# A Fourier transform with a soft mixture of experts behind it: one product of 128 columns along a, loads in halves, and another explicit order

## The chip, the core and the metric

The kernel runs on one core of a Trainium2 chip, in float32. The metric is the device time of one execution in microseconds. TensorE (PE; its weight loads are listed as PEld), VectorE (DVE), ScalarE (ACT), GpSimd (POOL) and SyncE (SP, which issues every DMA here) each work through a queue of their own in order and wait for each other by semaphores. Products go to PSUM, which has 8 banks of 512 floats per partition, and DVE or ACT have to copy them out.

## The reference

```python
x: (8, 2496, 256); phi: (256, 32); w1: (8, 256, 1024); w2: (8, 1024, 256)
x = np.fft.fft(np.fft.fft(x, axis=1), axis=2).real.reshape(19968, 256)
logits = x @ phi                                   # 19968 x 32 slots
d = softmax of logits over the 19968 tokens        # with + 1e-9 below the sum
slot_input = (d.T @ x).reshape(8, 4, 256)
slot_out[e] = np.maximum(slot_input[e] @ w1[e], 0) @ w2[e]
c = softmax of logits over the 32 slots            # with + 1e-9 below the sum
return c @ slot_out.reshape(32, 256)               # 19968 x 256
```

Nothing can be written before the last token has been read: the softmax over tokens needs the largest logit and the sum of all of them. So there is a stage that loads (x, then the expert weights) and one that stores.

## The kernel before

The 8 batches are worked in 4 pairs, p = 0 to 3. The 2496 tokens of a batch are 64 values a times 39 values c, so that the transform along the sequence is a small product along a and another along c. Step names below are a letter code and numbers (pair, tile or half), as they stand in `PLAN`, and each names a function.

- `X` (`load_x`) loads one of five tiles of x of a pair, 1 MB each (896 KB for the first), into one of six 1 MB homes R0 to R5. `XT` (`load_turned`) does it for a copy of pair 3 that is laid out turned. `F`, `G`, `H` (DVE, L302 and L313) fold a tile's mirrored tokens and features into a home E.
- `T` and `A` turn a tile on PE (L318) and copy it out of PSUM; `Zo`, `Ze`, `Zt` multiply with the phi tables (L333, L351), `Y` copies, `t` turns (L372), and `y` (`turn_z_copy`, L377) copies the turned z, slot by slot, into a home M.
- `a` (`along_a`, L394) is the product along a, `b` its copy, `l` (`along_c`, L410) the products with cosines and sines along c, in two halves of the groups. `L` copies the cosine product of a half, `M` and `N` (L428, DVE) add and subtract the sine product from PSUM: these are the logits.
- `R`, `V`, `v`, `vb`, `W`, `w` find each slot's largest logit of the pair, `E` (ACT, L463) the exponentials, `q` (DVE) their sums and differences. `e` (L480) and `d` (L494) go back along c and a, `u` (`inputs`, L522) multiplies with the folded x.
- After all four pairs `ac` (DVE), `acT`, `at`, `si`, `sT` put the slot inputs together, `h` (L610, w1), `r`, `x`, `s` (L628, w2), `so`, `rep` (L638) give the expert outputs. `I` and `J` load w1 (1 MB each, homes R) and w2 (512 KB each, homes E).
- For the outputs, `O` and `Q` (L648) turn the logits back to tokens, `ca`, `cb`, `cc`, `cd`, `ce` do the softmax over slots (DVE, ACT, some on POOL), `lT` and `lc` turn its weights (L693), `po` (`product`, L711) multiplies, `ev` copies out of PSUM into the homes R, and `S` (L723) stores 384 KB to 1 MB.

What sets the order is `PLAN` alone, a list of some 860 steps written out in full: it is walked once from front to back, each step issues its instructions on its engines, `/a`, `/v` or `/g` names the engine of a copy (ACT, DVE, POOL), and `=name:home` says which buffer a result takes. So an engine's queue has its steps in the list's order, and a load stands in SP's queue until the home that it names is free.

Of the kernel before, what the change touches and what calls it, by code (L numbers as in the profile page):

```python
# [8 lines left out]
F32 = mybir.dt.float32  # L9
# [8 lines left out]
D = 256  # L18
# [8 lines left out]

DIRECT = ()
# [5 lines left out]
X03=x03:R0 C0 F03 G03=e03:E0 T030=bT030:B0 X04=x04:R1 A030/a=et010:E1 H03 T031=bT031:B1 A031/a=et011:E2 X01=x01:R2  # L34
F04 G04=e04:E3 T040=bT040:B2 X00=x00:R3 H04 F01 A040/a=et020:E4 H01=e01:E5 T041=bT041:B3 T011=bT011:B4 C1
A041/a=et021:E6 A011/a=et001:E7 F00 P H00=e00:E8 phi=bphi:B5 T001=bT001:B6 A001/a wphi G01 Zo02=bz02:B7
T010=bT010:B0 A010/a=et000:E9 G00 T000=bT000:B1 Zo00=bz00:B2 X02=x02:R4 A000/a Ze00 F02 H02=e02:E10 T021=bT021:B3
A021/a G02 T020=bT020:B4 A020/a Ze02 X13=x13:R5 Zo01=bz01:B5 Ze01 Y02/a=zs0:M0 X14=x14:R0 C2 Y00/a F13 wneg
H13=e13:E11 G13 Y01/a t00=bt00:B6 y00/a=zt0:M1 t02=bt02:B0 X10=x10:R1 X11=x11:R2 y02/a F14 G14=e14:E12 H14
t01=bt01:B1 T130=bT130:B3 T131=bT131:B4 y01/a a02=ba02:B7 X12=x12:R3 F10 b02/a=oo0:M2 a01=ba01:B2 A131/a=et111:E13  # L40
b01/a a00=ba00:B5 A130/a=et110:E14 l01=bl01:B6,bm01:B0 L01/a=lt0:M3 X20=x20:R4 H10=e10:E15 T101=bT101:B1 b00/a
A101/a=et101:E16 T140=bT140:B7 T141=bT141:B4 A141/a=et121:E17 G10 A140/a=et120:E6 T100=bT100:B2 M01 F11 X21=x21:R5
N01 H11=e11:E7 l00=bl00:B3,bm00:B6 Zo12=bz12:B5 G11 Ze12 T111=bT111:B1 F12 O02=bc02:B4 L00/a A100/a=et100:E9 M00
Y12/a=zs1:M4 t12=bt12:B0 T110=bT110:B7 A111/a Zo10=bz10:B3 H12=e12:E4 X24=x24:R0 A110/a Ze10 X22=x22:R1 G12 Y10/a
T121=bT121:B2 X23=x23:R2 A121/a T120=bT120:B5 t10=bt10:B1 F20 N00 H20=e20:E2 Zo11=bz11:B7 A120/a Ze11 R01
O01=bc01:B3 y10/a=zt1:M5 y12/a Q02/a=c0:M6 T201=bT201:B2 Y11/a R00 t11=bt11:B6 y11/a V01=bv01:B5 O00=bc00:B1 G20
T200=bT200:B0 A200/a=et200:E1 XT30=xt30:R3 F24 Q01/a A201/a=et201:E17 Q00/a v01 V00=bv00:B4 vb01/a=me01:X0
a11=ba11:B7 v00 vb00/a=me00:X1 a10=ba10:B6 G24=e24:E6 b10/a=oo1:M7 b11/a H24 a12=ba12:B0 b12/a XT32=xt32:R4
XT34=xt34:R0 W01 T240=bT240:B3 A240/a=et220:E16 T241=bT241:B2 W00 l11=bl11:B1,bm11:B6 F21 F22 A241/a=et221:E9
L11/a=lt1:M8 w00/a l10=bl10:B7,bm10:B0 w01/a L10/a E001=d00:D0 Zo22=bz22:B3 G21=e21:E13 H21 Ze22 Y22/a=zs2:M9  # L50
H22=e22:E14 T211=bT211:B2 F23 A211/a M10 T221=bT221:B1 T210=bT210:B4 A210/a t22=bt22:B5 y22/a=zt2:M0 FT30 M11
Zo20=bz20:B7 H23=e23:E9 Ze20 Zt30=bz30:B3 E000 Y20/a A221/a=et211:E16 N11 XT33=xt33:R5 T231=bT231:B2 G22 N10 A231/a
t20=bt20:B4 T220=bT220:B5 XT31=xt31:R3 A220/a=et210:E17 O10=bc10:B7 O12=bc12:B6 O11=bc11:B1 G23 E011=d01:D1
Q11/a=c1:M1 R11 V11=bv11:B0 T230=bT230:B2 FT34 Zo21=bz21:B5 A230/a Ze21 Y21/a Zt34=bz32:B1 y20/a Q10/a Y32/a=zs3:M2
Q12/a E010 FT32 Zt32=bz31:B2 FT33 Zt33 Y31/a FT31 Zt31 Y30/a R10 V10=bv10:B5 v11 vb11/a=me11:X0 q010=q01:D2
t21=bt21:B4 t31=bt31:B7 v10 C3 q001=q00:D3 q011 ca00 vb10/a=me10:X1 t30=bt30:B1 y21/a y31/a=zt3:M4 y30/a cb00/v q000
C4 X31=x31:R1 W10 w10/a E100=d10:D1 W11 t32=bt32:B6 a21=ba21:B2 y32/v F31 E101 G31=e31:E1 J1=w21:E16 w11/v
q100=q10:D0 ca01 q101 a22=ba22:B3 b22/a=oo2:M5 b21/a a20=ba20:B4 b20/a e00=be000:B7,be001:B1 e01=be010:B5,be011:B6
# [36 lines left out]
po32=bp320:B1,bp321:B6,bp322:B4,bp323:B0 ev131/a S300 ev331/a ev320/v=o32:R0 ev323/a S110
po31=bp310:B3,bp311:B7,bp312:B5,bp313:B2 ev312/v=o31:R2 ev313/v ev311/a ev322/a
# [724 lines left out]
```

## Time and profile before

| | before |
|---|---|
| median of 3 runs | 183.2 us (182.17 to 184.05) |
| the profiled execution | 183.17 us, of it 181.4 us span from the first to the last instruction |
| busy: PE, DVE, ACT | 143.6, 127.0, 111.9 us |
| moved by DMA | 64.29 MB, mean 354 GB/s over the span |
| granted TensorE clock, mean | 0.918 |

The profile is one execution on the chip. The chain of waits is the work that ended last, followed back from the end: a piece is an engine's work, a DMA, or "issue", which is time in which the engine waited for nothing that the profile shows. A busy time is the union of an engine's instructions; PE's ends are modelled.

### The profile page before, as it was taken

What the parts mean: (1) busy time and instruction counts of PE and PEld (TensorE: products, weight loads), DVE (VectorE), ACT (ScalarE), POOL (GpSimd) and SP (SyncE); (2) the same over time, 40 slices, a digit from 0 to 9 for tenths busy, and PEclk for the clock granted to TensorE, in tenths of its full rate; (3) what the DMA queues carried; (4) which work ended last, traced back from release to release, by engine and by line L of the source; (5) the groups of instructions that cost most, each with busy time, mean ns of one, the idle gap of its engine ahead of it and who ended that gap; (6) DMA issues with size and microseconds to landing.
All of it is one profiled execution on the core that took longest, in us unless ns stands there. A gap on an engine that the chain in (4) does not pass through costs nothing.

```text
span 181.4 us, 5827 instructions
## 1 busy us (share of the span) xinstructions
PE 143.6 (79%) x2494; PEld 99.6 (55%) x2494; DVE 127.0 (70%) x222; ACT 111.9 (62%) x268; POOL 11.4 (6%) x24
## 2 busy tenths in 40 slices
PE   0279969998999993999963999999999989796000
PEld 0257658668788882766951386448575745342000
DVE  0699893998999794969977086997899777343000
ACT  2042677798997995879962453545877877545100
POOL 2000000000000000000000000002855000000000
PEclk9999999999999999999997599999999999955555
DMA  5999999999858999851799925799999999999994
GB/s 193 426 417 419 413 421 416 423 420 386 302 206 354 425 423 409 351 175 42 246 388 412 417 74 219 264 401 407 405 400 374 405 419 424 414 426 416 423 416 206
DMA packets 11546, 64.29 MB, mean 354 GB/s; under 512 B 1409, under 2 KB 1793, under 8 KB 6401
## 3 DMA queue, kind: packets, MB, share of 16 engines
q1 hardware_dynamic: 11520, 63.93, 88.2%
q8 instruction: 19, 0.31, 0.7%
q14 instruction: 7, 0.05, 0.1%
HBM read 43.48 MB, written 20.45 MB: 352 GB/s over the span
## 4 chain that ended last, share of the span: by engine, by line
PE 65%; DMA 9%; ACT 7%; issue 6%; DVE 4%; SPq 0%; ACTq 0%; DVEq 0%
PE B L711 10%; PE B L318 7%; PE B L494 6%; PE B L394 6%; DMA out<-R 6%; PE B L333 6%; PE B L522 5%; ACT M L235 5%; PE B L628 4%; PE B L610 4%; DMA R<-xh 4%; PE B L480 4%; PE B L410 3%; PE B L693 3%; PE B L648 2%
## 5 line engine op out<-in xcount | busy, mean ns | idle before, releaser
L235 ACT COPY M<-B 128x480 f32<-128x480 f32 (+11 forms) x101 | 44.2, 524 | 17.5 <-PE B L480 6.0
L235 ACT COPY R<-B 128x512 f32<-128x512 f32 (+1 forms) x49 | 25.3, 592 | 12.0 <-PE B L711 6.6
L711 PE MATMUL B<-E,rh 32*128 32x512 f32 (+2 forms) x192 | 29.8, 589 | 2.8 <-ACT R L235 1.6
L235 ACT COPY E<-B 128x512 f32<-128x512 f32 (+1 forms) x37 | 21.1, 583 | 16.4 <-PE B L318 15.1
L233 DVE COPY R<-B 128x512 f32<-128x512 f32 (+1 forms) x31 | 19.7, 664 | 12.9 <-PE B L711 6.9
L302 DVE TENSOR_TENSOR R<-R 128x1024 f32<-128x1024 f32 (+1 forms) x20 | 23.1, 1163 | 7.2 <-DMA R<-xh 6.9
L318 PE MATMUL B<-cs,E 128*128 128x128 f32 x120 | 20.1, 316 | 9.0 <-DVE E L313 9.0
L313 DVE TENSOR_TENSOR E<-R 128x512 f32<-128x512 f32 x40 | 26.2, 682 | 0.7 <-PE B L522 0.4
L711 PEld LDWEIGHTS B<-E,rh 32*128 32x128 f32 x192 | 15.4, 193 | 13.6 <-ACT R L235 8.6
L318 PEld LDWEIGHTS B<-cs,E 128*128 128x128 f32 x120 | 15.9, 162 | 12.2 <-DVE E L313 10.2
L463 ACT ACTIVATE D<-M,nm 124x128 f32<-124x128 f32 x44 | 14.2, 400 | 0.0
L480 PE MATMUL B<-cs,D 60*64 60x60 f32 x352 | 7.4, 222 | 7.3 <-issue 7.3
L394 PE MATMUL B<-cs,M 128*64 128x64 f32 x352 | 11.4, 223 | 2.2 <-issue 1.4
L428 DVE TENSOR_TENSOR M<-M,B 124x320 f32<-124x320 f32 (+1 forms) x16 | 8.0, 513 | 7.0 <-ACT M L235 6.9
L394 PEld LDWEIGHTS B<-cs,M 128*64 128x64 f32 x352 | 10.8, 138 | 4.0 <-issue 4.0
L333 PE MATMUL B<-E,wphi 128*32 128x256 f32 (+1 forms) x216 | 12.1, 359 | 0.0
L494 PE MATMUL B<-M,cs 128*32 128x320 f32 x128 | 11.9, 529 | 0.0
L687 POOL TENSOR_TENSOR M<-M,cm 128x640 f32<-128x640 f32 x5 | 6.3, 1264 | 86.7 <-DVE cm L682 86.7
L480 PEld LDWEIGHTS B<-cs,D 60*64 60x64 f32 x352 | 6.5, 135 | 8.5 <-issue 8.2
L522 PE MATMUL B<-E,M 128*32 128x129 f32 x320 | 9.9, 274 | 0.7 <-issue 0.7
L522 PEld LDWEIGHTS B<-E,M 128*32 128x32 f32 x320 | 8.8, 110 | 1.4 <-issue 0.9
L468 DVE TENSOR_TENSOR D<-D 124x320 f32<-124x320 f32 (+1 forms) x16 | 7.8, 512 | 1.8 <-ACT D L463 1.8
(94 smaller groups left out, 169.8 us busy)
## 6 DMA issues: line engine op xcount, KB each, us to landing
R<-xh SPq DMA_DIRECT2D x16, 1024.0 KB, 12.0
out<-R SPq DMA_DIRECT2D x12, 1024.0 KB, 9.6
E<-w2h SPq DMA_DIRECT2D x16, 512.0 KB, 8.1
R<-w1h SPq DMA_DIRECT2D x8, 1024.0 KB, 8.1
out<-R SPq DMA_DIRECT2D x9, 512.0 KB, 4.4
R<-xth SPq DMA_DIRECT2D x4, 1024.0 KB, 5.6
R<-xh SPq DMA_DIRECT2D x4, 896.0 KB, 11.9
out<-R SPq DMA_DIRECT2D x3, 896.0 KB, 6.6
```

The lines of the kernel that those rows point to most:

```text
L233: v.tensor_copy(dst, src)
L235: sc.copy(dst, src)
L302: v.tensor_tensor(x[:, lo], x[:, lo], x[:, hi], op=ALU.add)
L313: v.tensor_tensor(d, x[:, 0:4, 0:128], x[:, 0:4, 128:256], op=ALU.subtract if k else ALU.add)
L318: pe.transpose(b[:, g * 128 : g * 128 + 128], x[:, g, k * 128 : k * 128 + 128], ident)
L333: pe.matmul(z[32 * g : 32 * g + 32, o : o + n], wphi[:, w, :], turned_x(p, u, k)[:, g].rearrange("p h q a -> p (h q a)"), start=w != 0, st ...
L394: pe.matmul(d[64 * r : 64 * r + 64, h, i], z[:, 4 * b + i, h], C("wa")[:, 64 * r : 64 * r + 64], start=True, stop=True, tile_position=(0, ...
L463: sc.activation(d[:, g], L[:, g], AF.Exp, bias=nms[:, p, hf, g : g + 1], scale=1.0)
L480: pe.matmul(b[64 * k : 64 * k + 64, 60 * i : 60 * i + 60], q[rows, i, m if direct else k], C(tab)[rows], start=m == 0, stop=m == 1 or not ...
L494: pe.matmul(b[32 * c : 32 * c + 32, :320], C("wb")[:, 64 * k + 32 * (c % 2) : 64 * k + 32 * (c % 2) + 32], s[:, 16 * hf : 16 * hf + 16, c ...
L522: pe.matmul(b[32 * g : 32 * g + 32, 0:129], d[:, k, c, :], x[:, c % 4, 0:129] if k == 0 else x[:, c % 4, 127:256], start=cc == 0, stop=cc ...
L711: pe.matmul(view(f"bp{p}{b}{i}", 512)[:, q * n : q * n + n], rh[rows, dc], l[rows, :n], start=True, stop=True, tile_position=(32 * i, 0),)
```

## The change

The product along a is issued once for each group of three slots, over 128 columns of the whole table, where there were four products of 64 columns by 64. Its rows now hold the halves h, and its columns the cosine and sine parts r, so the products along c take their rows by h. The sine product lands with its halves exchanged; it is copied to SBUF, half by half, and the sums are made against the cosine product in PSUM. The copy of the turned z walks its columns so that runs of 8 (or 4) neighbours are written, and reads PSUM in steps instead. Loads of x, of the turned x and of w1 are halves of what they were, each a step of its own. Fourteen products of a tile of ones with itself (`dm`) are put at places of the list, and the list is another one throughout.

```diff
+WARM = (256, 256, 256, 256, 256, 256, 256, 256, 256, 256, 256, 256, 256, 256)
 PLAN = """
-X03=x03:R0 C0 F03 G03=e03:E0 T030=bT030:B0 X04=x04:R1 A030/a=et010:E1 H03 T031=bT031:B1 A031/a=et011:E2 X01=x01:R2
...
+dm11=bw11:B0 dm3=bw3:B1 dm13=bw13:B2 X011=x01:R0 C0 X010 X030=x03:R1 F01 H01=e01:E0 G01 X031 F03 G03=e03:E1
...
+        warm = const("warm", 128, max(WARM)) if WARM else None
...
+        def keep_warm(e, i):
+            n = WARM[i]
+            pe.matmul(view(f"bw{i}", 512)[:, :n], warm[:, :128], warm[:, :n], start=True, stop=True)
...
-        def load_x(e, p, t):
+        def load_x(e, p, t, h):
             r0, n = _rows(t)
-            nc.sync.dma_start(view(f"x{p}{t}", n * D), xh[p, :, r0 * D : (r0 + n) * D])
+            lo, hi = (0, 4) if h == 0 else (4, n)
+            nc.sync.dma_start(view(f"x{p}{t}", n * D)[:, lo * D : hi * D], xh[p, :, (r0 + lo) * D : (r0 + hi) * D])
...
+        def load_w1(e, i, h):
+            src = w1h[i // 4, i // 2 % 2, i % 2][:, 2 * h : 2 * h + 2]
...
-            d = z[:, :, :, :60].rearrange("p g h (s c) -> p h c g s", s=GS)[:, :, 8 * u : 8 * u + 4 * nq]
-            b = view(f"bt{p}{u}", 512)[:, : 256 * nq].rearrange("p (h i s) -> p h i s", h=2, s=NSLOT)
-            copy(e, d[:, :, :, : NG - 1], b[:, :, :, :30].rearrange("p h i (g s) -> p h i g s", s=GS))
-            copy(e, d[:, :, :, NG - 1, :2], b[:, :, :, 30:])
+            d = z[:, :, :, :60].rearrange("p g h (s c) -> p g s h c", s=GS)[:, :, :, :, 8 * u : 8 * u + 4 * nq]
+            b = view(f"bt{p}{u}", 512)[:, : 256 * nq].rearrange("p (h i s) -> p s h i", h=2, s=NSLOT)
+            copy(e, d[:, : NG - 1], b[:, :30].rearrange("p (g s) h i -> p g s h i", s=GS))
+            copy(e, d[:, NG - 1, :2], b[:, 30:])
 
         def along_a(e, p, b):
...
-                for h in range(2):
-                    for r in range(2):
-                        pe.matmul(
-                            d[64 * r : 64 * r + 64, h, i], z[:, 4 * b + i, h], C("wa")[:, 64 * r : 64 * r + 64],
-                            start=True, stop=True, tile_position=(0, 64 * r),
-                        )
+                g = 4 * b + i
+                pe.matmul(
+                    d[:, i * 128 : i * 128 + 128], z[:, g].rearrange("p h q -> p (h q)"), C("wa"), start=True, stop=True
+                )
...
         def along_c(e, p, hf):
             g0, n = GH[hf]
             for h in range(2):
+                rows = slice(64 * h, 64 * h + 60)
                 for r in range(2):
-                    o = view(f"oo{p}", 2, NG, NA)[64 * r : 64 * r + 60, h, g0 : g0 + n].rearrange("p u k -> p (u k)")
-                    b = view(f"b{'lm'[r]}{p}{hf}", 512)
+                    o = view(f"oo{p}", 2, NG, NA)[rows, r, g0 : g0 + n].rearrange("p u k -> p (u k)")
+                    b, c = view(f"b{'lm'[r]}{p}{hf}", 512), 64 * (h ^ r)
...
-        def along_c_copy(e, p, hf):
-            g0, n = GH[hf]
-            b = view(f"bl{p}{hf}", 512, rows=124)[:, : n * NA]
-            copy(e, logits(p, hf)[:, :, 0], b.rearrange("p (g n) -> p g n", g=n))
+        def along_c_copy(e, p, hf, h):
+            n = GH[hf][1]
+            lo, w = 64 * (1 - h), (64, 60)[h]
+            b = view(f"bm{p}{hf}", 512)[lo : lo + w, : n * NA]
+            copy(e, logits(p, hf)[64 * h : 64 * h + w, :, 0], b.rearrange("p (g n) -> p g n", g=n))
...
-            v.tensor_tensor(L[:, :, 1 - i], L[:, :, 0], b, op=ALU.subtract if i else ALU.add)
+            v.tensor_tensor(L[:, :, 1 - i], b, L[:, :, 0], op=ALU.subtract if i else ALU.add)
```

**How the order moves, on PE, where pair 0 starts its way back.** Before, PE's queue from the turned z of pair 3 (L372) through the product along a of pair 2 (L394) into the way back along c of pair 0 (L480):

```order
L453 MATMUL B_104<-cs_112,X_102 124x128
L372 MATMUL B_110<-cs_112,M_90 128x128 x2
L394 MATMUL B_106<-cs_114,M_88 64x64 x16
L394 MATMUL B_107<-cs_114,M_88 64x64 x12
L394 MATMUL B_108<-cs_114,M_88 64x64 x16
L480 MATMUL B_111<-cs_115,D_101 64x60 x2
L480 MATMUL B_105<-cs_115,D_101 64x60 x2
```

The last two rows repeat: both halves of pair 0's way back stand there in a row, 44 products in all, each of which is two matmuls in the profile.

After, on the same engine, around the first half of pair 0's way back (L490; L329 is `T`, L383 is `t`, L344 is `Zo` and `Ze`):

```order
L383 MATMUL B_111<-cs_112,M_97 128x128 x4
L329 MATMUL B_106<-cs_112,E_84 128x128 x4
L383 MATMUL B_109<-cs_112,M_97 128x128 x2
L329 MATMUL B_105<-cs_112,E_84 128x128 x4
L383 MATMUL B_104<-cs_112,M_88 128x128 x2
L344 MATMUL B_110<-E_87,wphi 32x256 x8
L344 MATMUL B_110<-E_83,wphi 32x256 x4
L490 MATMUL B_106<-cs_115,D_99 64x60 x2
L490 MATMUL B_108<-cs_115,D_99 64x60 x2
```

Only the first half, 24 products, stands there now, behind turns and products of other pairs; the second half follows some 180 matmuls later.

**On ACT, pair 0's turned z and logits.** Before, the six copies of `y` (M_89 from PSUM), those of the product along a, and the one copy that a half of the logits has (M_91):

```order
L235 COPY M_89<-B_110 128x2x8x10x3
L235 COPY M_89<-B_110 128x2x8x2
L235 COPY M_89<-B_104 128x2x4x10x3
L235 COPY M_89<-B_104 128x2x4x2
L235 COPY M_89<-B_105 128x2x8x10x3
L235 COPY M_89<-B_105 128x2x8x2
L235 COPY M_90<-B_111 128x2x192
L235 COPY E_83<-B_108 128x8x64
L235 COPY M_90<-B_106 128x2x256
L235 COPY E_84<-B_107 128x8x64
L235 COPY M_91<-B_110 124x5x64
```

After, from the second copy of `y` on:

```order
L242 COPY M_89<-B_104 128x10x3x2x4
L242 COPY M_89<-B_104 128x2x2x4
L242 COPY M_89<-B_106 128x10x3x2x8
L242 COPY M_89<-B_106 128x2x2x8
L242 COPY M_90<-B_109 128x2x256
L242 COPY M_90<-B_107 128x2x256
L242 COPY M_90<-B_105 128x2x192
L242 COPY M_91<-B_111 128x2x2x64
L242 COPY M_92<-B_106 64x6x64
L242 COPY M_92<-B_106 60x6x64
```

As many copies of `y` as before, with 8 or 4 neighbours innermost instead of 3 or 2 columns apart, and two copies for a half of the logits (M_92) where one was.

**On SP, the last loads before the stores.** Before, then after (L257 and L270 are w1, L262 and L273 w2):

```order
L257 DMA R_65<-w1h 128x2048
L257 DMA R_68<-w1h 128x2048
L257 DMA R_64<-w1h 128x2048
L257 DMA R_67<-w1h 128x2048
L262 DMA E_73<-w2h 128x1024
```

```order
L270 DMA R_69<-w1h 128x1024
L273 DMA E_79<-w2h 128x1024
L270 DMA R_66<-w1h 128x1024 x2
L270 DMA R_65<-w1h 128x1024 x2
L273 DMA E_76<-w2h 128x1024
```

A w1 load is now two of 512 KB; behind the last of w1 there were seven loads of w2, and there are six.

## Rows read from the trace of the kernel before

**Rows 1.** Busy time by stretch: start:end, length, busy us of each engine, clock, DMA share, GB/s.

```profile
0.00:126.30 126.30, 106.38 (x2148) 77.79 (x2149) 98.86 (x174) 82.58 (x211) 1.86 (x17) 0.97 0.86 337
126.30:181.40 55.10, 37.22 (x348) 21.84 (x348) 28.13 (x49) 29.36 (x58) 9.57 (x8) 0.79 0.97 394
70.00:80.00 10.00, 8.15 (x221) 6.33 (x221) 5.83 (x11) 6.28 (x18) 0.00 (x0) 1.00 0.74 282
90.00:100.00 10.00, 5.54 (x184) 4.00 (x179) 7.64 (x14) 4.63 (x13) 0.00 (x0) 0.86 1.01 395
100.00:110.00 10.00, 10.00 (x216) 6.41 (x208) 4.38 (x8) 5.36 (x14) 0.00 (x0) 0.80 0.63 242
```

**Rows 2.** SP's timeline, the last loads and the stores: start, us, line, tiles, count.

```profile
116.21 8.22 SPq L262 DMA_DIRECT2D E<-w2h  x7
128.22 43.14 SPq L723 DMA_DIRECT2D out<-R  x25
```

**Rows 3.** The chain of waits in order of time: start, us, what.

```profile
25.29 1.40 issue
26.68 2.79 PE B L394 x88
...
38.36 1.28 ACT M L235 x3
...
59.29 1.40 ACT M L235 x5
...
66.88 1.42 PE B L480 x85
68.30 2.85 issue
...
80.35 3.91 PE B L494 x56
...
91.50 1.52 PE B L522 x45
93.02 1.42 PE B L480 x83
94.44 3.80 issue
...
98.71 7.06 PE B L494 x64
...
126.29 2.00 PE B L711 x16
```

**Rows 4.** The page's DMA queues: packets, MB, share of 16 engines.

```profile
q8 instruction: 19, 0.31, 0.7%
...
HBM read 43.48 MB, written 20.45 MB: 352 GB/s over the span
```

**Rows 5.** ACT by form, 23.1 to 27.5 us, pair 0's turned z: count, busy us, mean ns.

```profile
L235 ACT COPY M<-B 128x480 f32<-128x480 f32 x2 | 2.5, 1266 | 0.0
L235 ACT COPY M<-B 128x240 f32<-128x240 f32 x1 | 0.8, 781 | 0.0
```

**Rows 6.** ACT by form, 111.9 to 115.5 us, turned logits; then a half of the logits.

```profile
L235 ACT COPY M<-B 128x480 f32<-128x480 f32 x2 | 1.1, 565 | 0.0
L235 ACT COPY M<-B 128x240 f32<-128x240 f32 x1 | 0.4, 361 | 1.5 <-PE B L648 1.5
...
L235 ACT COPY M<-B 124x384 f32<-124x384 f32 x4 | 1.9, 478 | 0.2 <-PE B L410 0.2
```

**Rows 7.** The chain of waits, dense runs of 128-by-128 matmuls, turn and product.

```profile
34.79 0.44 PE B L318 x4
...
125.53 0.29 PE B L638 x2
```

**Rows 8.** Busy time by stretch as above: loads of 512 KB, then stores of 1 MB.

```profile
122.00:127.00 5.00, 4.96 (x118) 4.13 (x114) 4.05 (x8) 2.75 (x5) 1.07 (x1) 1.00 1.01 401
160.00:170.00 10.00, 6.30 (x17) 2.22 (x14) 3.27 (x5) 3.90 (x8) 0.00 (x0) 0.50 1.01 421
```

**Rows 9.** What DVE's folds waited for, in total, times, longest.

```profile
DVE R L302 <- DMA R<-xh: 6.9, 3, 5.8
```

More of the change, by code (lines that the diff above doesn't have):

```diff
@@ L39 @@
[L39 to L58, printed above, removed]
@@ new lines @@
+l01=bl01:B4,bm01:B7 Zo11=bz11:B2 A130/a Ze11 L011/a X101 F10 L010/a Y11/a M00 G10=e10:E4 H10 T100=bT100:B6
+T101=bT101:B5 X110=x11:R3 X111 F11 H11=e11:E6 G11 t11=bt11:B3 A101/a=et101:E7 N00 M01 T111=bT111:B1 A111/a
+T110=bT110:B7 O00=bc00:B2 R00 A110/a=et100:E9 A100/a Zo10=bz10:B5 Ze10 V00=bv00:B0 y11/a Y10/a N01 X240=x24:R4
+X201=x20:R5 X200 F20 v00 vb00/a=me00:X0 G20=e20:E5 O02=bc02:B1 Q02/a=c0:M6 H20 O01=bc01:B7 t10=bt10:B6 y10/a Q00/a
+X211=x21:R0 X210 X241 F21 F24 G21=e21:E2 W00 T200=bT200:B4 T201=bT201:B3 A200/a=et200:E13 a10=ba10:B5 b10/a=oo1:M7
@@ new lines @@
+Y31/a b22/v l20=bl20:B3,bm20:B4 L200/a=lt2:M9 v11 vb11/a=me11:X1 L201/a l21=bl21:B6,bm21:B5 L210/a q010=q01:D0 q011
+X301=x30:R1 e01=be010:B1,be011:B7 f011/a L211/a f010/a X340=x34:R3 X341 F34 q101=q10:D1 W11 t31=bt31:B0 y31/a
+G34=e34:E7 M20 w11/v q100 E111=d11:D2 t30=bt30:B4 y30/a E110 N20 d000=bd000:B7 D000/a d011=bd011:B2 D011/a
+d010=bd010:B5 D010/a M21 e10=be100:B1,be101:B3 R20 V20=bv20:B0 f100/a=es1:M2 X311=x31:R4 a31=ba31:B4 b31/a=oo3:M4
+N21 R21 a32=ba32:B6 f101/v J0=w20:E17 X331=x33:R5 X320=x32:R2 q110=q11:D0 v20 H34 q111 ca00 vb20/a=me20:X0
@@ new lines @@
+a30=ba30:B7 b32/a V21=bv21:B2 W20 l31=bl31:B3,bm31:B5 X321 e11=be110:B1,be111:B4 C4 J1=w21:E13 w20/v X300 b30/a
+L311/v=lt3:M5 l30=bl30:B6,bm30:B7 u00=bu0:B0 u01 u02 u03 u04 L310/a f110/a f111/a L300/a M31 N31 v21 L301/a
+vb21/a=me21:X1 E201=d20:D3 E200 d101=bd101:B5 d100=bd100:B1 R31 V31=bv31:B4 W21 D100/a=ds1:M0 D101/a w21/a U0/a
+E210=d21:D1 X330 X310 I21=w12:R0 M30 N30 O31=bc31:B3 R30 q200=q20:D2 V30=bv30:B7 q201 e20=be200:B6,be201:B1
+f200/a=es2:M3 I40=w14:R3 E211 F32 d110=bd110:B5 d111=bd111:B2 v30 v31 vb31/a=me31:X0 H32=e32:E8 D110/a
@@ new lines @@
+s14 po02=bp020:B1,bp021:B7,bp022:B0,bp023:B4 lc10/v=ls10:E2 ev023/a=o02:R5 ev022/a J15=w215:E5 J13=w213:E13 ev020/a
+s15 ev021/a cb11/g ce31/g cd30 po10=bp100:B3,bp101:B2,bp102:B4,bp103:B6 ev101/v=o10:R3 s16 s17 ev100/a S001
+lT02=bl02x:B0 dm6=bw6:B1 so1/a ev102/a ev103/v rep1=br1:B7 dm7=bw7:B2 lc02/a=ls02:E9 rh1/a ce20/v cd21
+po04=bp040:B3,bp041:B5,bp042:B6,bp043:B1 po01=bp010:B4,bp011:B0,bp012:B7,bp013:B2 ev041/a=o04:R4 ev043/a
+ev011/a=o01:R2 ev042/v S000 ev040/v ev010/v ev013/v lT32=bl32x:B6 lc32/v=ls32:E0
@@ new lines @@
+po03=bp030:B5,bp031:B1,bp032:B3,bp033:B0 ev012/a cc11 ev033/a=o03:R1 cd11 ev031/v S021 lT20=bl20x:B4 ev030/a
+lc20/a=ls20:E11 ev032/a dm0=bw0:B7 dm10=bw10:B2 po34=bp340:B6,bp341:B0,bp342:B7,bp343:B5 ev340/a=o34:R0
+po21=bp210:B2,bp211:B4,bp212:B1,bp213:B3 ev342/a ev343/a S020 ev341/v ev210/a=o21:R5 ev212/v ev213/v ce30/g
+dm1=bw1:B6 po20=bp200:B0,bp201:B7,bp202:B5,bp203:B6 S100 ev202/a=o20:R3 S041 ev200/a ce11/g ce21/v ev203/v
+lT22=bl22x:B1 S010 lT30=bl30x:B2 ev211/v lc22/a=ls22:E1 S011 S040 S030 S031 po24=bp240:B3,bp241:B5,bp242:B6,bp243:B0
@@ new lines @@
+ev242/v=o24:R2 ev240/a dm9=bw9:B1 lT11=bl11x:B4 ev241/a lc30/a=ls30:E12 S340 ev201/a S210 S200 lT12=bl12x:B1
+lT31=bl31x:B6 dm2=bw2:B3 lT21=bl21x:B5 ev243/v po31=bp310:B0,bp311:B2,bp312:B3,bp313:B7 lc21/a=ls21:E3
+lc11/v=ls11:E6 lc12/v=ls12:E4 ev312/a=o31:R4 ev310/a ev313/a dm8=bw8:B4 lc31/v=ls31:E10 S240 ev311/v
+po32=bp320:B1,bp321:B6,bp322:B5,bp323:B4 ev320/a=o32:R1 ev321/a po12=bp120:B3,bp121:B2,bp122:B0,bp123:B7
+ev123/a=o12:R0 ev121/a ev323/v ev322/v ev122/v ev120/v po13=bp130:B1,bp131:B4,bp132:B6,bp133:B5 ev131/a=o13:R5
@@ new lines @@
+ev132/a ev130/v po14=bp140:B7,bp141:B0,bp142:B2,bp143:B3 ev142/a=o14:R3 ev141/v ev143/a ev140/v
+po11=bp110:B4,bp111:B1,bp112:B6,bp113:B2 ev110/v=o11:R2 S120 ev112/a ev113/v dm12=bw12:B0 dm4=bw4:B3
+po23=bp230:B7,bp231:B0,bp232:B6,bp233:B3 ev230/v=o23:R0 S140 S310 ev111/a ev133/a S130
+po30=bp300:B1,bp301:B4,bp302:B5,bp303:B2 ev302/v=o30:R3 ev301/v ev231/a ev232/a ev303/a ev233/a S230
+po33=bp330:B0,bp331:B6,bp332:B7,bp333:B2 ev332/v=o33:R4 ev333/a ev331/a po22=bp220:B3,bp221:B2,bp222:B5,bp223:B6
@@ L101 @@
+ev330/a ev223/a=o22:R5 S330 S110 S320 ev222/a ev300/a ev220/a ev221/a S300 S220
 """.split()
@@ L401, in along_a_copy @@
             s, d = view(f"ba{p}{b}", 512)[:, : 128 * n], view(f"oo{p}", 2, NG, NA)
-            copy(e, d[:, :, 4 * b : 4 * b + n], s.rearrange("p (h u k) -> p h u k", h=2, u=n))
+            copy(e, d[:, :, 4 * b : 4 * b + n], s.rearrange("p (u r k) -> p r u k", u=n, r=2))
         def along_c(e, p, hf):
@@ L406, in along_c @@
             for h in range(2):
+                rows = slice(64 * h, 64 * h + 60)
                 for r in range(2):
-                    o = view(f"oo{p}", 2, NG, NA)[64 * r : 64 * r + 60, h, g0 : g0 + n].rearrange("p u k -> p (u k)")
-                    b = view(f"b{'lm'[r]}{p}{hf}", 512)
+                    o = view(f"oo{p}", 2, NG, NA)[rows, r, g0 : g0 + n].rearrange("p u k -> p (u k)")
+                    b, c = view(f"b{'lm'[r]}{p}{hf}", 512), 64 * (h ^ r)
                     pe.matmul(
-                        b[64 * h : 64 * h + 64, : n * NA], C(("wcc", "wcs")[r])[64 * r : 64 * r + 60], o,
-                        start=True, stop=True, tile_position=(64 * r, 64 * h),
+                        b[c : c + 64, : n * NA], C(("wcc", "wcs")[r])[rows], o,
+                        start=True, stop=True, tile_position=(64 * h, c),
                     )
@@ L746, in _build @@
         with tc.manual_schedule():
+            if WARM:
+                gp.memset(warm, 1.0)
             gp.memset(mneg, 0.0)
@@ L754, in _build @@
                     at_home[name] = home[where_]
-                args = [int(i) for i in parts] if kind != "J" else [int(parts)]
+                args = [int(i) for i in parts] if kind not in ("J", "dm") else [int(parts)]
                 kinds[kind](e, *args)
```

108 lines of the change are left out of this document (46 added, 62 removed).

## The prediction

> **What bounds the kernel now.** I read the busy times by stretch first. They split at 126.3 us, where the first product for the outputs starts [rows 3]. Behind it the 16 DMA engines are busy 0.97 of the time [rows 1]: the stores go out from 128.22 us on [rows 2], 20.45 MB [rows 4], and at the 421 GB/s of a stretch of stores [rows 8] that is 48.6 us of the 53.2 that are left of the span; most of the rest is late w2, issued from 116.21 us on. So the end is the first store plus a fixed amount, and PE (37.2 us busy of 55.1), DVE (28.1) and ACT (29.4) have room there. What the change is worth is what it does to the first product.
>
> Up to 126.3 us nothing is full: PE 106.4 us, DVE 98.9, ACT 82.6, DMA 0.86 [rows 1]. The chain of waits tells where the time between goes. Three kinds of piece in it are not PE's own work:
> - PE waits for ACT around the turned z: 1.40 us at 25.29 (listed as "issue", but ACT's copies of pair 0's turned z end there), and further pieces near 38 and 59 us [rows 3].
> - PE stops for 2.85 us at 68.30 and 3.80 us at 94.44, both in the middle of the way back along c (L480), behind matmuls of the same step that wait for nothing [rows 3].
> - After the second stop the clock falls: the granted mean is 0.86 and 0.80 in the two stretches around it [rows 1], and 64 matmuls of L494 take 7.06 us where 56 took 3.91 before [rows 3]; 64 at that pace are 4.47, so 2.6 us are lost.
>
> I take the two stops for instruction fetch. PE's instructions come by DMA: queue q8 moved 0.31 MB in 19 packets [rows 4], 16.3 KB each, and 2494 matmuls ([rows 1], two of them counted in both stretches) with as many weight loads are 262 instructions, 131 matmuls, per packet. By the order of before, the stops lie 637 matmuls apart, 4.9 packets. And each comes where PE runs fastest: the last 128 matmuls before the first are 85 of L480 in 1.42 us and 43 of L394 at 2.79/88 us, 2.78 us together; before the second, 45 of L522 in 1.52 us and 83 of L480 in 1.42, 2.94 us [rows 3]. With the stop, a packet needed 5.6 and 6.7 us there, with the data queue full (share 1.01 in the stretch with the second, [rows 1]).
>
> The Trainium skill, "Runtime: NRT & Kernel Launch", section "Instruction fetch mechanics", says that blocks of 256 instructions are fetched by the sequencer's own queue while the current one runs, and that this is hidden by the issue floor. The packet size agrees; that it is hidden does not fit these stops. By the page they have another cause, which is a rival below.
>
> **Part by part.**
>
> *Turned z in runs.* The copy of 480 columns takes 1266 ns and that of 240 takes 781 [rows 5], while copies of the same shapes that write neighbours and read PSUM in steps, as the new form does, take 565 and 361 [rows 6]. I take the latter: 0.70 and 0.42 us less, 12 copies, 7.3 us of ACT. On the path are pair 0's three (1.8 us, but the wait was 1.4), two of 480 and one of 240 in the piece near 38 (1.8), and three of 480 near 59 (2.1): 5.3 us. The bounds are 0, should it be the reading in long steps that costs, and 5.3. I take 5.3 since only the write side differs between the two groups of rows.
>
> *Sine products copied in halves.* 16 copies instead of 8, 0.48 us each [rows 6]: +3.8 us of ACT, net -3.5 with the above. The sums wait for both halves, so on the path it is one such copy at pair 1 and one at pair 3, about -0.9 us; bounds 0 and -3.8.
>
> *Product along a.* 88 matmuls in 2.79 us per pair [rows 3] become 22 of full size. At the pace of the turns, 0.44/4, these are 2.42 us, and at that of the only 128-by-128 product, 0.29/2, 3.19 [rows 7]: over four pairs from 1.5 us gained to 1.6 lost. I take +1.0, nearer to the turns, since they too stand in a run. More weighty are 264 matmuls fewer, that is two packets of instructions.
>
> *The stops.* The order decides here. In the list after, matmul 983 (the first stop's) has 128 matmuls ahead of it that are 5.8 us of PE at the paces above (products along a, turns, half a way back), not 2.8: that stop is covered. Matmul 1620 falls among `k` and `si`, with 3.5 us ahead of it, mostly L522: up to 6.7 - 3.5 = 3.2 us remain, where PE waits for DVE's gather anyway; I leave 1.5. With 0.4 for the first, of 2.85 + 3.80 + 2.6 = 9.2 us some 7.3 are won. Bounds: 0 (both return) to 9.2.
>
> *Loads in halves.* A fold needs both halves, so nothing starts sooner. In a stretch of 512 KB loads DMA moves 401 GB/s at a share of 1.01, against 421 [rows 8]: 5%. Up to about 45 us loads follow each other without a gap, so at most 2 us; but behind the first tile DVE's folds waited 6.9 - 5.8 = 1.1 us for them in all [rows 9], so I take -0.5. The Trainium skill speaks against this edit: "DMA: Bandwidth & Descriptors", section "Bandwidth", wants transfers of 1 MiB and more, and fits about 2 us fixed per transfer. If that stood in line, 33 more transfers would be 66 us; the rows at 401 GB/s show transfers overlapping, so my sum doesn't use it.
>
> *Products of ones.* Four stand ahead of the first turn, while PE waits for the first tile: nothing. Ten stand at the expert outputs or later: 20 matmuls at 0.11 to 0.145 us, 2.2 to 2.9 us of PE behind or beside the first products, where DMA is the bound. Nothing, and if that cover were gone 2.9. The clock in the stretch before them they cannot change.
>
> *DVE's queue.* By steps of the list DVE does 2.5 us more ahead of the first product (two copies of turned x, a copy of weights, two subtractions of softmax maxima; others left). That is no delay by itself, but it is the next limit.
>
> **The sum.** 5.3 - 0.9 + 1.0 + 7.3 - 0.5 = 12.2 us earlier by the terms. I do not take all of it, since with these waits gone DVE is next. It was idle 126.3 - 98.9 = 27.4 us: 5.8 for the first tile [rows 9], 4.2, 2.4 and 5.6 in the three stretches with the stops and the slow clock [rows 1], and 9.4 in small waits that I let stand. Then the first product can't come before 98.9 + 2.5 + 5.8 + 9.4 = 116.6, 9.7 us earlier. The loads are 43.5 MB [rows 4], at 401 GB/s 108 us, so DMA too has only some 8 us left to wait for free homes. I take 118.6, 7.7 us earlier: **175.5 us** for the profiled execution (183.17), which is the median (183.2) within 0.1.
>
> **Rivals.**
> - *More.* All of the 12.2 us comes, DVE's small waits shrinking with ACT's load: 171. For it: ACT has 7 us less to do ahead of the first product. Against: PE, DVE and DMA would all be nearly full at once.
> - *The stops are not fetch*, as the page has it, and stay with the way back along c, which is as long as before: 12.2 - 7.3 = 4.9 us, or 178.3 to 180. Against: they came in two of eight ways back, five packets apart.
> - *The next limit takes all.* DVE's 2.5 us, the halved loads (up to 2 us) and pair-by-pair waits of the new order fill what ACT and PE gave: within 1%, 181.4 to 185.
> - *Slower.* The stops return at worse places: the list after has a run of both halves of pair 3's way back with L522 behind, 128 matmuls in 3.0 us, and one from L522 to the first w1 products in 3.1. If a packet ends in each with the queue full, that is 6.7 - 3.0 and 6.7 - 3.1, and 2.6 to 3.3 us of half clock behind each: 13.3 against 9.2 now, 4 us more; the full clock of the products along c would go as well. With the strided reads costing what the strided writes did (5.3 not won), the sine copies on the path (up to 3.8) and the loads' 2 us it is 187 to 191. It decides from about 3 us of new stops on, if ACT's gain fails too.
> - *The change doesn't do what it says:* the reads of PSUM in steps of 128 bytes could cost as the writes did; then the 5.3 us go, and 179 to 181 is left. I count it with the second rival.
>
> **How the numbers follow.** A difference of 1% (1.8 us) is about what a measurement of this kernel can tell from no change. Chances: forecast (173 to 178.2) 0.46, more (under 173) 0.14, fetch or strided reads otherwise (178.3 to 181.3) 0.14, the next limit takes all 0.14, slower 0.12. Faster by over 1%: 0.46 + 0.14 + 0.14 = 0.74; within 0.14; slower 0.12. The range 171 to 184.5 leaves out the slower case and the ends of two others, about 0.18.
>
> **What would show it.** The 480-column copies of the turned z near 0.57 us; the products along a near 2.4 us per pair; no "issue" of over 1 us within the way back along c, and a granted clock of 1.00 up to the first product; that product near 118 to 119 us with DVE over 100 us busy before it; 17 or 18 packets on q8; DMA at 0.97 behind it and stores of the same length. I am wrong if the copies stay over 1 us, if PE stops again where L522 and the ways back meet, or if the first product moves and the end doesn't.

## The result and the profile after

| | before | after |
|---|---|---|
| median of 10 runs | 183.0 us (181.91 to 185.68) | 180.92 us (176.53 to 181.99) |
| ratio after/before | | 0.9703 (0.9619 to 0.9787) |
| second set, 6 runs | 183.14 us | 181.14 us (180.4 to 183.79), ratio 0.9887 (0.9840 to 0.9933) |
| profiled execution | 183.17 us, span 181.4 | 181.21 us, span 179.3 |

The first ratio rests on the two shortest of the ten executions, since the others were counted as disturbed; the medians of all ten, and the second set, give 0.989, and I take that: some 2 us faster. The forecast was 7.7 us faster.

Busy time by stretch after (start:end, length, busy us of PE, PEld, DVE, ACT and POOL, clock, DMA share, GB/s), cut at the gather (where PE starts to put the slot inputs together, L571 before and L581 after) and at the first product, to be held against [rows 1]:

```profile
0.00:102.50 102.50, 89.41 (x1596) 67.09 (x1596) 85.27 (x142) 70.45 (x192) 1.67 (x17) 0.97 0.97 369
102.50:123.75 21.25, 17.54 (x348) 11.08 (x347) 16.88 (x35) 8.44 (x21) 5.51 (x4) 1.00 0.77 278
123.75:179.30 55.55, 37.37 (x323) 20.60 (x322) 27.22 (x51) 30.20 (x61) 3.79 (x3) 0.84 0.91 371
```

and the same two stretches of before, up to the gather and from there to the first product:

```profile
0.00:110.60 110.60, 90.76 (x1853) 68.67 (x1853) 84.83 (x140) 75.30 (x192) 1.49 (x16) 0.97 0.86 340
110.60:126.30 15.70, 15.62 (x297) 9.12 (x296) 14.03 (x34) 7.29 (x19) 0.37 (x1) 1.00 0.82 320
```

The gather starts 8.2 us earlier than before (102.5 against 110.7), and up to it DMA has been busy 0.97 of the time, against 0.86 before. Then 5.7 of these go again: the way to the first product takes 21.25 us where it took some 15.6, and PE, which had next to no idle time there, now waits 3.7. The rest to the end is as long as before (55.6 against 55.1).

The chain of waits after, from where PE stopped before to the gather and on (start, us, what):

```profile
83.88 0.92 issue
...
88.66 0.96 PE B L490 x53
89.62 3.17 issue
92.79 0.81 PE B L490 x35
93.60 1.02 PE B L532 x16
94.62 3.32 PE B L504 x32
...
103.65 1.53 issue
...
106.75 0.93 PE B L620 x6
...
108.46 10.24 DMA R<-w1h
118.70 0.04 issue
118.74 1.06 PE B L620 x8
```

Of the two stops in [rows 3] the first is gone. PE stops in pair 3's way back still (now L490), but after 53 matmuls, 3.17 us long, with a granted clock of 0.67 from 92.79 to 97.94 us: 32 matmuls of L504 take 3.32 us where 16 took 1.1. By the count of matmuls, which the shift below explains, this is not the second stop of before; that one is the 1.53 us at the slot inputs. And the last product with w1 waits for a load, by PE's list of waits:

```profile
PE B L620 <- DMA R<-w1h: 1.9, 1, 1.9
```

The copies of the turned z of pair 0 (ACT by form, 22 to 29 us: count, busy us, mean ns), the counterpart of [rows 5], and the queues of the page, of [rows 4]:

```profile
L242 ACT COPY M<-B 128x480 f32<-128x480 f32 x2 | 1.1, 562 | 0.0
...
L242 ACT COPY M<-B 128x240 f32<-128x240 f32 x1 | 0.4, 363 | 0.0
```

```profile
q1 hardware_dynamic: 16272, 63.94, 91.8%
q8 instruction: 18, 0.29, 0.6%
```

The copies are as fast as was read from [rows 6]. The data queue's packets took 91.8% of 16 engines over 179.3 us, 164.6 us; before it was, in the same place of the page:

```profile
q1 hardware_dynamic: 11520, 63.93, 88.2%
```

88.2% of 181.4 us, 160.0: the same bytes in 4.6 us more. The row of before was on the page from the start, and the prediction left it unread.

### The profile page after: what moved, and what is told of

Same layout as the page of the kernel before. It is cut to its first block, busy times and chain, and to the rows that moved or that the text cites. A ratio compares the mean times of both kernels' runs of the same rounds, so it can differ in the third digit from the quotient of the medians.

```text
span 179.3 us, 5424 instructions
## 1 busy us (share of the span) xinstructions
PE 144.3 (80%) x2258; PEld 98.8 (55%) x2258; DVE 129.4 (72%) x227; ACT 109.1 (61%) x272; POOL 11.0 (6%) x24
## 3 DMA queue, kind: packets, MB, share of 16 engines
q1 hardware_dynamic: 16272, 63.94, 91.8%
## 4 chain that ended last, share of the span: by engine, by line
PE 52%; DMA 21%; ACT 7%; DVE 5%; issue 5%; SPq 2%; ACTq 0%; DVEq 0%
DMA R<-xh 10%; PE B L721 10%; DMA R<-w1h 6%; DMA out<-R 5%; PE B L504 5%; PE B L403 5%; PE B L532 4%; PE B L344 4%; PE B L329 4%; ACT M L242 3%; PE B L490 3%; PE B L362 3%; PE B L703 2%; ACT R L242 2%; PE B L638 2%
## 5 line engine op out<-in xcount | busy, mean ns | idle before, releaser
L242 ACT COPY M<-B 128x320 f32<-128x320 f32 (+14 forms) x107 | 42.3, 443 | 17.3 <-PE B L490 4.5
L721 PE MATMUL B<-E,rh 32*128 32x512 f32 (+2 forms) x192 | 26.3, 551 | 1.8 <-ACT R L242 1.5
L242 ACT COPY E<-B 128x512 f32<-128x512 f32 (+1 forms) x34 | 18.4, 590 | 14.1 <-PE B L329 13.4
L329 PE MATMUL B<-cs,E 128*128 128x128 f32 x120 | 17.9, 289 | 7.0 <-DVE E L324 7.0
L329 PEld LDWEIGHTS B<-cs,E 128*128 128x128 f32 x120 | 13.8, 147 | 11.5 <-DVE E L324 10.6
L721 PEld LDWEIGHTS B<-E,rh 32*128 32x128 f32 x192 | 12.2, 183 | 9.4 <-ACT R L242 5.7
L344 PE MATMUL B<-E,wphi 128*32 128x256 f32 (+1 forms) x216 | 11.8, 348 | 0.1
L504 PE MATMUL B<-M,cs 128*32 128x320 f32 x128 | 11.5, 479 | 0.1
L248 PE MATMUL B<-warm 128*128 128x256 f32 x28 | 10.0, 473 | 1.1 <-POOL warm L758 1.1
L403 PE MATMUL B<-cs,M 128*128 128x128 f32 x88 | 10.7, 276 | 0.0
L490 PE MATMUL B<-cs,D 60*64 60x60 f32 x352 | 7.5, 222 | 3.8 <-issue 3.6
L403 PEld LDWEIGHTS B<-cs,M 128*128 128x128 f32 x88 | 10.2, 192 | 0.2 <-issue 0.2
L490 PEld LDWEIGHTS B<-cs,D 60*64 60x64 f32 x352 | 6.5, 135 | 6.2 <-issue 4.2
L676 DVE TENSOR_REDUCE cm<-M 128x20 f32<-128x640 f32 x8 | 6.3, 806 | 4.8 <-ACT M L242 4.8
L620 PE MATMUL B<-R,sT 128*32 128x512 f32 x64 | 7.8, 596 | 1.9 <-DMA R<-w1h 1.9
```

What stands on the lines that cost most here:

```text
L242: sc.copy(dst, src)
L329: pe.transpose(b[:, g * 128 : g * 128 + 128], x[:, g, k * 128 : k * 128 + 128], ident)
L344: pe.matmul(z[32 * g : 32 * g + 32, o : o + n], wphi[:, w, :], turned_x(p, u, k)[:, g].rearrange("p h q a -> p (h q a)"), start=w != 0, st ...
L403: pe.matmul(d[:, i * 128 : i * 128 + 128], z[:, g].rearrange("p h q -> p (h q)"), C("wa"), start=True, stop=True)
L490: pe.matmul(b[64 * k : 64 * k + 64, 60 * i : 60 * i + 60], q[rows, i, m if direct else k], C(tab)[rows], start=m == 0, stop=m == 1 or not ...
L504: pe.matmul(b[32 * c : 32 * c + 32, :320], C("wb")[:, 64 * k + 32 * (c % 2) : 64 * k + 32 * (c % 2) + 32], s[:, 16 * hf : 16 * hf + 16, c ...
```

## The experiments

Each was run beside the kernel before. "Changed" below is the changed kernel.

**The changed kernel again** (no edit). 

> The changed kernel once more, as the base for the others. In the profile shown of it the gather stood 8.2 us earlier than before (102.50 against 110.74 us) and the end only 2.1 us. If that execution is typical, 180 to 181 us and a ratio of 0.985 to 0.99; if the executions of 176.5 and 178.6 us among the ten are what it does undisturbed, 177 to 178 us.

181.14 us, 0.9887 (0.9840 to 0.9933): the first case. Its profile has the gather at 104.40 us and stops of 1.19 and 3.99 us in the chain, but only 0.10 at the slot inputs, and the first product at 123.02: the 21.25 us from gather to product are 18.6 here. One profile alone does not say where time is lost to within 2 or 3 us.

**Whole loads.** (The cut shows steps picked out of longer lines of the list, as do the cuts below.)

```diff
-X011=x01:R0 C0 X010
+X01=x01:R0 C0
...
-I21=w12:R0
-I20
+I2=w12:R0
```

> The changed kernel with x, turned x and w1 loaded whole again (1 MB), each load where its first half stood. Theory (the halves cost DMA time, and DMA is now short of it): the data queue's share of 16 engines' span falls from 164.6 us to about 160, and 2 to 4.5 us of the time come back (176.5 to 179 where the changed kernel has 181). Rival (DMA waits for homes and for compute, so cheaper packets only make longer gaps): the share falls alike, the time stays within 1 us.

176.67 us, 0.9632 (0.9592 to 0.9672): 4.5 us less than the changed kernel, its theory's upper end. Queue and stops of this kernel, by the page and the chain:

```profile
q1 hardware_dynamic: 11520, 63.93, 90.7%
```

```profile
86.76 0.96 PE B L486 x53
87.72 0.97 issue
88.69 0.79 PE B L486 x35
89.49 0.58 PE B L528 x16
90.06 2.15 PE B L500 x32
92.22 1.31 PE B L528 x45
93.52 1.37 issue
...
99.55 2.08 issue
```

and the stretch up to the gather:

```profile
0.00:98.41 98.41, 88.36 (x1597) 67.20 (x1597) 84.96 (x142) 70.29 (x192) 1.68 (x17) 1.00 0.97 388
```

90.7% of 175.1 us is 158.8 us of DMA, some 6 us less than the 164.6 with halves. Up to the gather DMA is as busy as with halves (0.97) and moves 388 GB/s instead of 369. The stop after the same 53 matmuls is 0.97 us instead of 3.17 and 3.99, but two more follow, and in sum these stops are 4.4 us, against 5.6 and 5.3 in the two profiles with halves. No wait for w1 is left in PE's list. The gather is at 98.41 us, 4.1 and 6.0 earlier than in those two, and the first product at 119.66, 4.1 and 3.4 earlier.

**Other homes for the last w1 blocks.**

```diff
-I60=w16:R2
-I61
-I71=w17:R1
-I70
-J7=w27:E6
+I60=w160:E8
+I61=w161:E7
+I71=w171:E16
+I70=w170:E6
+J7=w27:R2
```

> The changed kernel with the last two w1 blocks loaded into four homes E that are free before the gather, where they waited for the homes R that the first expert products free; the w2 block of that home goes to R2. Theory (the 5.7 us between gather and first product went to this wait): the issue at 106.65 us moves to about 100, h111 no longer waits for a load, the first product comes 2 to 5 us earlier, and so does the end. Rival (PE's own work there, 17 us of it by the list, is the bound): the loads land earlier, the first product stays within 1 us.

179.62 us, 0.9794 (0.9752 to 0.9837): 1.5 us less than the changed kernel. In SP's timeline the loads were issued from 102.17 us on instead of 106.65, and the only wait for w1 left in PE's list is one of 0.3 us at a weight load. In the chain, though, PE works through from 106.98 us to the first product at 123.50:

```profile
104.62 2.36 issue
106.98 0.24 PE B L517 x8
...
111.20 3.57 PE B L619 x32
114.77 2.19 PE B L637 x80
116.96 0.86 PE B L619 x8
```

So the rival holds for the first product in this profile: after the gather PE's own work is the bound, together with a stop that is 2.36 us here. The profiled execution is the longest of the six (180.92 us), and I can't place the gain of the others in it.

**No products of ones** (`WARM = ()`, the `dm` steps left out). 

> The changed kernel without the fourteen products of ones. Theory (they stand beside the bound): within 0.7 us of the changed kernel either way, the clock the same up to the first product. Rival (they hold the clock up between the first products): 1 to 3 us slower, with the clock at half somewhere between 120 and 155 us. Second rival (their 10 us of PE delay the products): 1 to 2 us faster.

181.66 us, 0.9825 (0.9764 to 0.9887), against 181.14 and 0.9887: no difference that can be told. PE is busy 143.5 us, against 147.3 in the second profile of the changed kernel and 144.3 in the first. The granted clock is 1.00 from 120 to 150 us with and without these products; from 150 to 155 it is 0.88 without them and 1.00 in the second profile with them, so the first rival's sign comes late, and without a cost that can be told. The run has a by-product. Eight matmuls fewer stand ahead of pair 3's way back, and the stop there comes after 61 matmuls instead of 53, eight later in the program:

```profile
91.02 1.07 PE B L487 x61
92.10 2.52 issue
94.61 0.67 PE B L487 x27
```

**A shift by 40 matmuls, in the kernel before.**

```diff
 PLAN = """
+dm0=bw0:B0 dm1=bw1:B1 dm2=bw2:B2
...
+dm19=bw19:B3
 X03=x03:R0 C0 F03
```

> The kernel before with 20 products of ones of 32 columns (40 matmuls) put ahead of all else, while PE waits for the first tile. Theory (the stops are the ends of instruction blocks): they keep their place in the count of matmuls, 983 and 1620, and so come 40 matmuls earlier in the program: after 45 of the way back of pair 0 where it was after 85, and after 43 of that of pair 3 where it was after 83. Rival (something in the way back along c stops PE): they stay at 85 and 83. Time within 2 us of before.

182.64 us, 1.0009 (0.9977 to 1.0042). Both stops moved by exactly 40 matmuls, against 85 and 83 in [rows 3]:

```profile
65.32 0.84 PE B L489 x45
66.16 2.75 issue
...
92.43 0.83 PE B L489 x43
93.26 3.10 issue
```

The stops keep their place in the count of instructions, whatever step stands there. The other traces say the same. This is how many matmuls PE had behind it at each stop of over 0.6 us in the chain that waited for nothing the profile shows:

| kernel | matmuls ahead of the stops |
|---|---|
| before | 983, 1110, 1492, 1620 |
| before, shifted | 983, 1492, 1620, 2127 |
| changed, first and second profile | 1235, 1363, 1619; 1235, 1363 |
| changed, whole loads | 1363, 1491, 1619 |
| before, with both edits | 1237, 1364 |

Within four matmuls, and a few records can be missing from a trace, all lie on one grid of steps of 128 (979, 1107, 1235, 1363, 1491, 1619, ...). The two stops of [rows 3] are five steps apart. One step ahead of the second, 45 and 83 matmuls before it, stands a stop of the kernel before that [rows 3] leaves out:

```profile
90.84 0.66 issue
```

With whole loads, above, it is 35, 16, 32 and 45 matmuls from stop to stop, again 128. That the stops depend on the count and not on the step is shown. That PE waits there for an instruction block is inferred, from this count and from queue q8, which brings one packet of 16 KB for some 131 matmuls over the whole run ([rows 4]): each stop of 0.9 us or more has one of these packets inside it or starting up to 1.6 us ahead of it.

**Loads in halves alone, in the kernel before.**

```diff
-X03=x03:R0 C0
+X030=x03:R0 X031 C0
...
-I1=w11:R5
+I10=w11:R5 I11
```

> The kernel before with nothing changed but the loads of x, turned x and w1, each issued as two halves in the same place. Theory (halves cost: 5% per byte, and they keep the queue full so that instruction blocks come later): 3 to 5 us slower than before, the two stops of PE in the way back along c (2.85 and 3.80 us) longer by 1 us or more in sum. Rival (the cost belongs to the new order alone): within 1 us of before.

186.55 us (182.78 to 187.35) against 182.81: 3.7 us slower by the medians. Five of the six took 186.0 to 187.35 us, but one took 182.78, as long as the kernel before, so what halves cost in the old order is not settled. In the profile, of 186.72 us, DMA's share over 10 to 40 us is 1.03 at 407 GB/s where it was 1.02 at 419, pair 0's product along a starts at 27.78 us instead of 26.68, and the three stops of 2.85, 0.66 and 3.80 us are 3.90, 1.80 and 3.25:

```profile
68.39 1.42 PE B L482 x84
69.81 3.90 issue
...
93.92 1.80 issue
...
98.67 3.25 issue
```

**Turned z in runs alone, in the kernel before** (`turn_z_copy` of the change). 

> The kernel before with the turned z written in runs, nothing else. Theory: its 480-column copies fall from 1266 to about 570 ns, and as three places of the chain wait for them it is 2 to 5 us faster. Rival (reads of PSUM in long steps cost as the writes did): copies over 1000 ns, no change. Second rival (other waits take over): copies at 570 ns, within 1 us.

180.61 us, 0.9894 (0.9844 to 0.9944): 1.9 us by the ratio, just below the theory's range. The copies are at 605 ns. In the profile, of 179.99 us, pair 2's product along a starts 4.4 us earlier than before (59.67 against 64.09), so most of the predicted waits went:

```profile
62.61 1.42 PE B L480 x85
64.03 3.90 issue
...
88.16 1.80 issue
...
92.90 3.25 issue
```

Then the stops take 0.9 us more in sum than the four of before, and the first product comes 3.3 us earlier (123.00 against 126.29). These are the stops of the kernel with halves, to the hundredth, and here the loads are whole. So the traces do not bear out the theory there that halves bring the blocks later.

**The product along a alone, in the kernel before.** First with the banks as they stood:

```diff
-l01=bl01:B6,bm01:B0 L01/a=lt0:M3
+l01=bl01:B6,bm01:B0 L010/a=lt0:M3 L011/a
```

> The kernel before with the product along a over 128 columns and the products along c and their copies that go with it (two copies for a half of the logits), nothing else. 2494 - 264 = 2230 matmuls, two instruction blocks fewer. Theory: L394's step takes about 2.4 us of PE per pair, the copies cost ACT 3.8 us, the stops move to other steps since the blocks end elsewhere; -2 to +2 us. Rival (fewer instructions are what the gain is about): 3 us or more faster.

186.36 us, 1.0232 (1.0195 to 1.0268). In it the differences (`N`) read a bank that a later step may have filled, so one half of the logits holds other numbers, and its waits are not those of the edit; its time says nothing about the edit. With the banks exchanged:

```diff
-l01=bl01:B6,bm01:B0 L01/a=lt0:M3
+l01=bl01:B0,bm01:B6 L010/a=lt0:M3 L011/a
```

> The kernel before with the product along a over 128 columns, as in b_a, with the banks of the cosine and sine products exchanged so that the one that is freed early is the one copied to SBUF. Theory: PE's step falls to about 2.4 us per pair, ACT has 3.8 us more, the stops come 132 matmuls earlier in the program's steps; -2 to +2 us against before. Rival (264 matmuls fewer are the gain): 3 us or more faster. Second rival (the second copy and the sum from the other bank lengthen the way to the largest logits): 3 us or more slower, as b_a was.

182.31 us, 0.9996 (0.9967 to 1.0025): nothing, inside the theory. 22 matmuls take 2.69 us in the chain of pair 0, no less than the 88 did within 0.1, and the stops are 1.55 and 2.91 us, two packets having gone from q8 (17). The stop of 2.85 us is gone, yet pair 3's way back starts no sooner than before (89.17 against 89.06 us): ACT's work fills the chain from 65 to 77 us instead.

**Both edits, with the order of before and whole loads.** 

> The order of before with both the product along a of b_a2 and the turned z in runs, and loads whole: what of the change is not order, halves or products of ones. The changed kernel with whole loads took 176.7 us. Theory (the order is worth 3 to 4 us of that): 180 to 181. Rival (order is worth nothing, the two edits do it): 176 to 178.

177.65 us, 0.9719 (0.9673 to 0.9766), inside the rival's range: 5.1 us by the ratio, where the two alone give 1.9 and 0.1. Part of the difference is that the blocks end elsewhere: the stops of over 0.6 us in its chain are 3.4 us shorter in sum than the four of before:

```profile
85.43 1.74 issue
...
90.55 2.91 issue
```

**x whole, w1 in halves** (the `X` and `XT` part of the whole loads alone). 

> The changed kernel with x and turned x loaded whole and w1 still in halves. Theory (the halves cost by their bytes, 25.6 MB of x and 8.4 MB of w1): three quarters of the 4.4 us come back, about 177.5 to 178. Rival (they cost through full queues where the late w1 loads meet PE's instruction blocks): under 1.5 us comes back, 179.5 to 181.

178.41 us, 0.9671 (0.9607 to 0.9735): by medians 2.7 of the 4.5 us come back, by the ratios 85%, and by the interval 60% or more. Most of the cost is in the loads of x, where most bytes are; how much the halves of w1 cost on their own is inside the intervals.

**Whole loads and the other homes.** 

> The changed kernel with x, turned x and six of the eight w1 blocks whole, and the last two w1 blocks as halves in homes E that are free early. Whole loads gave 4.4 us and the homes 1.5. If they add up: 175 to 175.5. If both work on the same wait: 176 to 177.

176.51 us, 0.9611 (0.9556 to 0.9667), against 176.67 without the homes: the two do not add up, as when both work on the same waits. Either of these beats both kernels, by 3.7 to 3.9% and 2.5 to 2.8%.

Put one after another, by the ratios, the two edits are worth -5.1 us, the order and the products of ones -1.6 (from 0.9719 to 0.9632, intervals that just touch), and the halves +4.7 (from 0.9632 to 0.9887). Each step starts where the last ends, so that these add up to the measured -2.0 checks nothing; what each is worth in another order of steps was not run.

## Why the prediction was right in sign and too large

- **Turned z in runs: right.** 562 and 363 ns against 565 and 361 predicted. Of the 5.3 us forecast on the path, 4.4 were there at pair 2's product along a when it ran alone, and 1.9 at the end. That both edits together give 5.1 is no check of the 5.3: that kernel's stops are shorter too.
- **Sine copies and product along a: right within their bounds, too kind.** 0.48 and 0.42 us per copy; 22 matmuls in 2.46 us after (68.25 us in the chain) against 2.42 taken. Together they moved nothing (0.9996), where the sum had +0.1, and that is partly luck: the stop of 2.85 us went with them and pair 3's way back started no sooner, so up to there they cost some 3 us, an estimate from these numbers.
- **Loads in halves: the step that failed.** The prediction has "behind the first tile DVE's folds waited 6.9 - 5.8 = 1.1 us for them in all [rows 9], so I take -0.5", at most 2. It measured 4.7 in the changed order. The sum looked for a wait of the folds, but the cost lies in DMA's own time. In the changed order DMA is short all the way to the gather, busy 0.97 of the time with halves (369 GB/s) and with whole loads (388), where it had 0.86 in the order of before. The prediction's "some 8 us left to wait for free homes" were not left once the data queue needed 4.6 us more. Its 5% was a comparison of loads with stores; loads against loads it is 3% (407 against 419 GB/s). By one profile each, the first product comes 4.1 us earlier with whole loads: about 1.2 of it were there at 83 us (82.69 against 83.88), 1.2 are shorter stops, and 1.9 the wait for w1 that is gone. This split is argued and not shown.
- **The stops: cause borne out, sum wrong.** They follow the count, with 128 matmuls to a block and not the 131 worked out there. Of 9.2 us 7.3 were to be won. The first stop is gone, as predicted, and the one at `k` and `si` left 1.53 us where 1.5 was left standing. That agreement is luck: the same stop is 0.10 us in the second profile and 2.08 with whole loads. The step took only the two block ends that had stopped PE before. Two others, after 1235 and 1363 matmuls, now stopped it for 0.92 and 3.17 us. From the end of the first to the end of the second, a block took 8.0 us (8.8 in the second profile), not the 5.6 to 6.7 on which the step rested. With the slow clock, some 6.7 us of 9.2 remain. The prediction had this place among its signs of being wrong: a stop "where L522 and the ways back meet".
- **From gather to product: not in the sum.** The 7.7 us were there at the gather (8.2). The sum counted steps of before up to the first product and missed what the new list puts ahead of it: 1.9 us more work of PE, and w1 loads that wait for homes R until 106.65 us. The homes took the wait away and the first product hardly moved (123.50, against 123.75 and 123.02). Since the stop there is anything from 0.10 to 2.36 us, these profiles show the extra work and can't price the load.
- **The stage of stores: right.** 55.6 us against 55.1, at a DMA share of 0.91 instead of the 0.97 expected. The products of ones cost nothing that can be told, though a pass of their 256 columns takes 0.215 us and not the 0.11 to 0.145 taken. DVE's 102 us up to the first product are the 101.4 predicted, and it was not the limit.

By its number the measured time, 180.9 and 181.1 us, falls to the second rival (178.3 to 181.3). Its mechanism is refuted: the stops follow the count, and the strided reads are fast. By mechanism it is nearer to "the next limit takes all" (181.4 to 185), with DMA and the halved loads as that limit. The Trainium skill, "DMA: Bandwidth & Descriptors", section "Bandwidth", asks for transfers of 1 MiB and more. The runs here agree with its direction: 407 GB/s where whole loads had 419. The fixed 2 us for each transfer stand in that page of the Trainium skill in another section, "Anatomy of one DMA — SWDGE (gpsimd) path", for DMAs that GpSimd issues. SP issued these, and nothing like the 66 us that the prediction worked out from it shows. The Trainium skill, "Runtime: NRT & Kernel Launch", section "Instruction fetch mechanics", has the fetch hidden. The runs here show stops of up to 4 us that follow the count of instructions; if they are the fetch, as inferred above, it is not hidden here, and the measurement decides.

## What to carry to other kernels

Before a load is cut into smaller ones, take the data queue's total from the page, not the waits for loads: where an edit elsewhere is to make the kernel shorter, the DMA time that is idle now can be used up by it, as it was here. On an engine that streams thousands of small instructions, count instructions as well as time: an idle that no semaphore explains, at a fixed place in the count, points to an instruction block that came late, and a shift by a few dummy instructions tells whether it follows the count or the step. Edits that take work off the path may show little alone and more together, since the next wait in line can depend on where such a block ends. Where such stops differ between two profiles of one kernel by up to 1.5 us, as here, take more than one profile before you put a gain of that size down to a place.

## What the runs showed of the hardware

ACT copies that read PSUM in steps of 128 bytes and write runs of 8 take 562 ns for 480 columns, near the pace of those of 512 columns (586), while those that write to SBUF in steps of 80 bytes take 1266. A matmul of 128 by 128 in a row of such costs 0.11 us per pass, as much as three or four of 64 by 64, so the larger form saves instructions and hardly time. Loads of 512 KB (4 KB per partition) moved 407 GB/s where loads of 1 MB (8 KB) moved 419. PE stopped after 45 and 43 matmuls of a step once 40 were put ahead of the program, where it had been 85 and 83, and in six traces of five kernels its stops lie within four matmuls of a grid of 128.
